# An LRU scan gated by a GEGLU network on one core: the engine orders are planned anew, with a charge between dependent neighbours on one engine

## The chip, the cores and the metric

The kernel runs on one core of a Trainium2 chip. The core's engines work side by side, each through its own queue, in order: TensorE (PE in the profile; its weight loads are PEld), VectorE (DVE), ScalarE (ACT) and GpSimd (POOL); SyncE (SP) issues most of the DMAs, ScalarE and GpSimd issue a few. Engines wait for one another on semaphores. The metric is the device time of one execution in microseconds, lower is better; of several runs the median is taken.

## The reference

`x` is 2048 tokens of 512 numbers in bfloat16. The reference normalizes it, sends it through a complex diagonal recurrence (512 states, one step per token) and through a GEGLU network of width 1376, and joins the two with `x`:

```python
def _A_ref(x, Lambda_re, Lambda_im, B_re, B_im, C_re, C_im, log_dt, Dskip):
    Lam = Lambda_re + 1j * Lambda_im
    Bmat, Cmat = B_re + 1j * B_im, C_re + 1j * C_im
    dt = jnp.exp(log_dt)
    Lam_bar = jnp.exp(dt * Lam)
    B_bar = ((Lam_bar - 1.0) / Lam)[:, None] * Bmat
    Bu = jnp.einsum("bld,pd->blp", x + 0j, B_bar)
    h = jnp.zeros_like(Bu[:, 0, :])
    hs = []
    for t in range(L):
        h = Lam_bar[None, :] * h + Bu[:, t, :]
        hs.append(h)
    hseq = jnp.stack(hs, 1)
    return 2.0 * jnp.einsum("blp,dp->bld", hseq, Cmat).real + x * Dskip[None, None, :]

def _B_ref(x, w_gate, w_up, w_down):
    return (_gelu(x @ w_gate) * (x @ w_up)) @ w_down

xn = _layernorm(x, axis=-1)
s = _A_ref(xn, ...)
g = _silu(_B_ref(xn, ...))
return x + s * g
```

## The kernel before, in words

**Tiles and stages.** The 2048 tokens are cut into four stretches (s = 0 to 3) of 512, each of four tiles (m) of 128 tokens. For each stretch the kernel makes:

- the normalized tile xn and its transpose xnT. For s = 0 and 1 VectorE takes statistics (`stats`, L375 and L377; `rstd`, L383; GpSimd's power, L380; `norm_dve`, L417); for s = 2 and 3 ScalarE sums x and its square (L764, into junk), VectorE works out four small operations (L769 to L772) and nb (L775), and ScalarE writes xn (L746). The transposes of s = 0 go through TensorE (L398, evicted by ScalarE, L401), those of the other stretches through SP's DMA queue (L423);
- the gate and up products (TensorE, L450 for s = 0, L471 after), evicted by ScalarE as gelu (gt) and copy (ub), multiplied by VectorE into at (L457; L489 and L491), transposed by DMA into atT (L497);
- the state input (L573), in two halves of the states, evicted by ScalarE into U (L576); then on VectorE, for each half: Q = U times a table of cosines and sines (L587), W = sum of two parts of Q (L599; L595 for s = 0), four real scans Fs (L606), the carry ini (L616 to L619), Q = Fs times the table (L587) and hst (L599). This turns the complex recurrence into real scans in a rotating frame;
- the down product from atT and wd (L514), evicted by ScalarE through silu into g (L518);
- the y product from hst and C (`y_tile`, L533). It is accumulated in one of two PSUM banks (ybank). Before it ScalarE writes the skip term sk (made by VectorE, L427) into the bank as the start value (L529, the seed); the first two y tiles have no seed and add sk on VectorE (L543, tF). VectorE multiplies the bank by g (L539 yg; L545 for the first two), adds x (L547 ot), and SP sends ot out (L550). A bank may be seeded for its next tile once yg (or tF) has read it.

TensorE has three more double banks in PSUM (slot), taken in turn by gate and up, state and down products. It may write a bank again when ScalarE has evicted it.

**The order.** The kernel is written as a list of steps, each with an engine, a cost, what it reads and writes. `Plan` orders them: some passes of list scheduling, then 3000 trials with random changes of the starts (seeded, so the same list always gives the same order), each judged by a model: every engine takes one step after the other, a step begins when what it needs is ready, and the best order by `goal` is what the program then issues. TensorE's steps are chained to one another and keep the order in which they are written. The cost of a VectorE step is `base + n / 960 / rate`, with 0.072 for `base` where nothing is given. A step that depends on another engine's step begins that step's lag later (0.13 for VectorE, 0.15 for ScalarE, 0.22 for TensorE); one that depends on its own engine's step begins when that ends:

```python
def _same(self, i, u):
    a, b = min(i, u), max(i, u)
    return a in self.steps[b][8] or (self.steps[a][0] == self.steps[b][0] and self.steps[a][0] in (PE, DVE, ACT, POOL))
...
    e = t + cost + (0.0 if same else lag if forward else self.steps[u][4])
```

No step of the plan is timed at run time: the plan's costs decide the order alone.

Of the kernel before, what the change touches and what calls it, by code (L numbers as in the profile page):

```python
# [13 lines left out]
ALU = mybir.AluOpType  # L14
# [6 lines left out]
PE, ACT, DVE, POOL, SP, ACTQ = "PE", "ACT", "DVE", "POOL", "SP", "ACTQ"  # L21


class Plan:
# [9 lines left out]
    def add(self, eng, cost, emit, reads=(), writes=(), lag=0.05, table=None, not_before=0.0, rank=0.0, after=()):  # L34
        n = len(self.steps)
        deps = set()
        for k in reads:
            if k in self.wrote:
                deps.add(self.wrote[k])
        for k in writes:  # L40
            if k in self.wrote:
                deps.add(self.wrote[k])
            deps.update(self.read.get(k, ()))
        deps.update(after)
        if eng == PE:
            if self.last_pe is not None:
                deps.add(self.last_pe)
            self.last_pe = n
        for k in reads:
            self.read.setdefault(k, []).append(n)  # L50
        for k in writes:
            self.wrote[k] = n
            self.read[k] = []
        deps.discard(n)
        self.steps.append((eng, cost, emit, sorted(deps), lag, table, not_before, rank, frozenset(after)))
        return n

    def _same(self, i, u):

        a, b = min(i, u), max(i, u)  # L60
        return a in self.steps[b][8] or (self.steps[a][0] == self.steps[b][0] and self.steps[a][0] in (PE, DVE, ACT, POOL))

    def _pass(self, into, prio, forward):


        n = len(self.steps)
        out = [[] for _ in range(n)]
        for i in range(n):
            for d in into[i]:
                out[d].append(i)  # L70
        left = [len(into[i]) for i in range(n)]
        ready_at = [self.steps[i][6] if forward else 0.0 for i in range(n)]
        waiting = {}
        free = {}
        loaded = None
        start = [None] * n
        for i in range(n):
            if left[i] == 0:
                waiting.setdefault(self.steps[i][0], []).append(i)
        done = 0  # L80
        length = 0.0
        while done < n:
            t, eng = min((max(free.get(e, 0.0), min(ready_at[i] for i in w)), e) for e, w in waiting.items() if w)
            w = waiting[eng]
            ahead = LOOK if eng in (DVE, ACT, POOL) else 1e-9

            def value(i):
                v = prio[i] - HOLD * max(0.0, ready_at[i] - t)
                table = self.steps[i][5]
                if table is not None and table != loaded:  # L90
                    v -= TABLE
                return (v, -i)

            i = max((j for j in w if ready_at[j] <= t + ahead), key=value)
            w.remove(i)
            t = max(t, ready_at[i])
            cost, lag, table = self.steps[i][1], self.steps[i][4], self.steps[i][5]
            if table is not None and table != loaded:
                loaded = table
                cost = cost + 1.3  # L100
            start[i] = t
            free[eng] = t + cost
            length = max(length, t + cost + (lag if forward else 0.0))
            done += 1
            for u in out[i]:
                same = self._same(i, u)
                e = t + cost + (0.0 if same else lag if forward else self.steps[u][4])
                ready_at[u] = max(ready_at[u], e)
                left[u] -= 1
                if left[u] == 0:  # L110
                    waiting.setdefault(self.steps[u][0], []).append(u)
        return start, length

    def _decode(self, users, key):

        n = len(self.steps)
        left = [len(s[3]) for s in self.steps]
        ready_at = [s[6] for s in self.steps]
        heap = [(key[i], i) for i in range(n) if left[i] == 0]
        heapq.heapify(heap)  # L120
        free = {}
        loaded = None
        start = [0.0] * n
        length = 0.0
        while heap:
            i = heapq.heappop(heap)[1]
            eng, cost, _, _, lag, table = self.steps[i][:6]
            t = max(free.get(eng, 0.0), ready_at[i])
            if table is not None and table != loaded:
                loaded = table  # L130
                t = max(t, free.get(eng, 0.0) + 1.3)
            start[i] = t
            free[eng] = end = t + cost
            length = max(length, end + lag)
            for u, same in users[i]:
                e = end if same else end + lag
                if e > ready_at[u]:
                    ready_at[u] = e
                left[u] -= 1
                if left[u] == 0:  # L140
                    heapq.heappush(heap, (max(key[u], key[i]), u))
        return start, length

    def run(self):
        n = len(self.steps)
        deps = [s[3] for s in self.steps]
        users = [[] for _ in range(n)]
# [2 lines left out]
                users[d].append(i)  # L150
        tail = [0.0] * n
        for i in range(n - 1, -1, -1):
            eng, cost, lag = self.steps[i][0], self.steps[i][1], self.steps[i][4]
            tail[i] = cost + max((tail[u] + (0.0 if self._same(i, u) else lag) for u in users[i]), default=0.0)
        rank = [s[7] for s in self.steps]
        best = None
        prio = tail
# [12 lines left out]
            back, _ = self._pass(users, [start[i] + self.steps[i][1] for i in range(n)], False)  # L170
            prio = [back[i] + self.steps[i][1] for i in range(n)]
        rng = random.Random(1)
        pairs = [[(u, self._same(i, u)) for u in users[i]] for i in range(n)]
        for r in range(TRIALS):
            key = list(best[1])
            if r:
# [16 lines left out]
def kernel(  # L193
# [34 lines left out]
    MAGIC = 12582912.0  # L228
# [3 lines left out]
    V, A, G, T = nc.vector, nc.scalar, nc.gpsimd, nc.tensor  # L232
# [33 lines left out]
    sk = [sb(f"sk{i}", [P, M, D]) for i in range(2)]  # L266
    NG2 = 3
    g2 = [sb(f"g2_{i}", [P, 2, D], FP32) for i in range(NG2)]
    yg = [sb(f"yg{i}", [P, D]) for i in range(2)]
# [12 lines left out]
    def dve(n, emit, reads=(), writes=(), rate=1.0, base=DV, **kw):  # L282
        return pl.add(DVE, base + n / 960.0 / rate, emit, reads, writes, lag=0.13, **kw)
# [89 lines left out]
    def stats(s, m):  # L373
        def f():
            V.bn_stats(out=st[:, s, m, :], in_=x_tok[:, s * M + m, :])  # L375
        dve(512, f, [("x", s, m)], [("st", s, m)], base=0.1)
        dve(6, lambda: V.bn_aggr(out=mv[:, s, m, :], in_=st[:, s, m, :]), [("st", s, m)], [("mv", s, m)], base=0.17)  # L377

    def power(out, base, exponent, n, reads, writes):
        pool(0.45 + 0.2 * n, lambda: G.tensor_tensor(out=out, in0=base, in1=exponent, op=ALU.pow), reads, writes)  # L380

    def rstd(s, a, b):
        dve(b - a, lambda: V.tensor_scalar(out=ve[:, s, a:b], in0=mv[:, s, a:b, 1], scalar1=EPS, scalar2=None, op0=ALU.add),  # L383
            [("mv", s, m) for m in range(a, b)], [("ve", s, m) for m in range(a, b)], base=0.14)
        power(rs[:, s, a:b], ve[:, s, a:b], mhalf[:, a:b], b - a, [("ve", s, m) for m in range(a, b)] + ["mhalf"], [("rs", s, m) for m in range(a, b)])

    def dummies(k, i):
# [135 lines left out]
    def y_tile(s, m):  # L523
# [13 lines left out]
        gi, b = g2s[s, m]  # L537
        if seed:
            dve(512, lambda: V.tensor_tensor(out=yg[e][:], in0=bank[:], in1=g2[gi][:, b, :], op=ALU.mult),  # L539
                [("y", i), ("g2", gi)], [("yg", e)])  # L540
        else:
            ys = tF[:, i, :]
            dve(512, lambda: V.tensor_tensor(out=ys, in0=bank[:], in1=sk[s % 2][:, m, :], op=ALU.add),  # L543
                [("y", i), ("sk", s % 2, m)], [("tF",)])
            dve(512, lambda: V.tensor_tensor(out=yg[e][:], in0=ys, in1=g2[gi][:, b, :], op=ALU.mult),  # L545
                [("tF",), ("g2", gi)], [("yg", e)])
        dve(512, lambda: V.tensor_tensor(out=ot[e][:], in0=yg[e][:], in1=x_tok[:, s * M + m, :], op=ALU.add),  # L547
            [("yg", e), ("x", s, m)], [("ot", e)], rate=2.0)
        mg = s * TS + m * P
# [73 lines left out]
    def tables():  # L623
# [1 line left out]
        sh, ch = sb("sh", [P, NPT, NB]), sb("ch", [P, NPT, NB])  # L625
        sp, cp = sb("sp", [P, NPT, NA, 2]), sb("cp", [P, NPT, NA, 2])
        dve(196, lambda: V.tensor_tensor(out=ang[:], in0=iota_f[:].unsqueeze(1).to_broadcast(W3), in1=thn.unsqueeze(2).to_broadcast(W3), op=ALU.mult),
            ["iota", "thn"], ["ang"], base=0.13)
        dve(196, lambda: V.tensor_scalar(out=kr[:], in0=ang[:], scalar1=MAGIC, scalar2=MAGIC, op0=ALU.add, op1=ALU.subtract), ["ang"], ["kr"], rate=2.0, base=0.13)
        dve(196, lambda: V.tensor_tensor(out=ang[:], in0=ang[:], in1=kr[:], op=ALU.subtract), ["kr"], ["ang", "kr"], base=0.13)  # L630
        dve(196, lambda: V.scalar_tensor_tensor(out=kr[:], in0=ang[:], scalar=-1.0, in1=ang[:], op0=ALU.mult, op1=ALU.max), ["ang"], ["kr"], base=0.13)
        early.append(acts(196, lambda: act(out=sbt[:], in_=ang[:], func=AF.Sin, scale=TWO_PI), ["ang"], ["sbt"], table="silu", rank=20.0))
        early.append(acts(196, lambda: act(out=cbt[:], in_=kr[:], func=AF.Sin, scale=-TWO_PI, bias=halfpi[:]), ["kr", "halfpi"], ["cbt", "trig"], table="silu", rank=20.0))
# [218 lines left out]
```

## Time and profile before

| what | value |
|---|---|
| median of 8 runs | 184.9 us |
| fastest and slowest run | 183.1 and 185.41 us |
| the profiled execution, its own time | 183.19 us |
| its span, first to last instruction | 181.4 us |
| TensorE busy in the span | 174.3 us (96%) |
| VectorE busy | 159.2 us (88%) |
| ScalarE busy | 117.8 us (65%) |
| GpSimd busy | 11.9 us (7%) |
| mean granted TensorE clock | 0.996 |

The eight runs in order: 184.93, 183.1, 183.23, 185.41, 185.36, 184.87, 185.3, 183.26.

How to read the profile: a row of the timeline gives the start and the duration in us, the engine, the line of the kernel, the operation, out<-in by the kernel's names (buffer numbers left out), shapes, and how many instructions were merged. In brackets stands idle time of the engine ahead of the row and what ended it. The end of a matmul is modelled and overlaps the next one's start, so starts are what to go by. The two durations of VectorE's neighbours may overlap a little: the next one starts while the one ahead is finishing.

### The profile page before, as it was taken

Reading aid. Unit: us, or ns where it says so; the run is one execution under the profiler, and the core shown is the slowest. Engines: PE = TensorE matmul, PEld = TensorE weight load, DVE = VectorE, ACT = ScalarE, POOL = GpSimd, SP = SyncE. Lnnn points to the kernel's source line nnn. Section 1 sums busy time; section 2 is a strip of 40 time slices with the busy share of each in tenths; the row PEclk is TensorE's granted clock in tenths of the full one; section 3 lists DMA queues with packets and bytes.
Section 4 is the critical chain, followed back from the end, with each engine's and each line's share of the span. In section 5 each row is a group of like instructions: output and inputs, shape, how many; then the busy total and the mean of one; then the engine's idle time right before and its main releaser. Section 6 shows DMA issues by size and latency. Waiting matters only on the chain.

```text
span 181.4 us, 2388 instructions
## 1 busy us (share of the span) xinstructions
PE 174.3 (96%) x848; PEld 82.5 (45%) x848; DVE 159.2 (88%) x265; ACT 117.8 (65%) x178; POOL 11.9 (7%) x21
## 2 busy tenths in 40 slices
PE   6999999999999999999999999999999999799990
PEld 2454445544444545444444544444444545344440
DVE  5899899999999999999999999999999999840072
ACT  4599699698999998565289774347428666242220
POOL 5430331000000200000020000000000000000000
PEclk9999999999999999999999999999999999999998
DMA  4999999991000577400020673041000241830011
GB/s 123 376 305 227 361 146 242 267 230 25 0 0 0 98 146 102 91 0 0 9 79 33 124 148 68 14 83 60 29 29 0 57 88 32 155 102 5 0 58 58
DMA packets 46995, 18.01 MB, mean 99 GB/s; under 512 B 38440, under 2 KB 46984, under 8 KB 46984
## 3 DMA queue, kind: packets, MB, share of 16 engines
q1 hardware_dynamic: 46400, 17.34, 42.4%
q10 hardware_dynamic: 552, 0.53, 1.1%
q8 instruction: 6, 0.10, 0.2%
q14 instruction: 5, 0.04, 0.1%
q0 software_dynamic: 32, 0.00, 0.0%
HBM read 6.33 MB, written 2.10 MB: 46 GB/s over the span
## 4 chain that ended last, share of the span: by engine, by line
DVE 73%; PE 12%; issue 6%; DMA 3%; POOL 2%; ACT 1%; SPq 1%; DVEq 0%
DVE Fs L606 20%; DVE Q L587 18%; PE ybank L533 6%; PE slot L514 5%; DVE W L599 4%; DVE at L489 4%; DMA wu<-in_B_w_up_dram 3%; DVE hst L599 3%; DVE yg L539 3%; DVE sk L427 2%; DVE Q L647 2%; DVE at L457 2%; DVE ot L547 2%; DVE at L491 2%; DVE C L790 2%
## 5 line engine op out<-in xcount | busy, mean ns | idle before, releaser
L471 PEld LDWEIGHTS <-xnT 128*128 128x128 bf16 x288 | 28.2, 98 | 28.4
L514 PE MATMUL slot<-wd,atT 128*128 128x512 bf16 (+1 forms) x176 | 38.7, 379 | 0.0
L471 PE MATMUL slot<-wg,xnT 128*128 128x512 bf16 (+1 forms) x144 | 31.8, 357 | 0.0
L471 PE MATMUL slot<-wu,xnT 128*128 128x512 bf16 (+1 forms) x144 | 31.8, 357 | 0.0
L533 PE MATMUL ybank<-C,hst 128*128 128x512 bf16 x128 | 28.9, 379 | 1.3 <-ACT ybank L529 1.3
L606 DVE TENSOR_TENSOR_SCAN Fs<-rho,ini,W 128x512 bf16<-128x512 f32 x24 | 29.3, 1268 | 0.1
L573 PE MATMUL slot<-xnT,BT 128*128 128x512 bf16 x128 | 28.3, 379 | 0.0
L514 PEld LDWEIGHTS <-atT 128*128 128x128 bf16 (+1 forms) x176 | 17.2, 98 | 20.9
L576 ACT ACTIVATE U<-slot 128x1024 bf16<-128x1024 f32 x16 | 16.1, 1020 | 11.1 <-PE slot L573 11.1
L539 DVE TENSOR_TENSOR yg<-ybank,g 128x512 bf16<-128x512 f32 x14 | 9.7, 690 | 13.9 <-PE ybank L533 13.5
L529 ACT ACTIVATE ybank<-sk 128x512 f32<-128x512 bf16 x14 | 8.4, 601 | 18.2 <-DVE yg L539 17.1
L533 PEld LDWEIGHTS <-hst 128*128 128x128 bf16 x128 | 12.5, 98 | 15.8 <-issue 1.6
L573 PEld LDWEIGHTS <-BT 128*128 128x128 bf16 x128 | 12.5, 98 | 15.0
L587 DVE TENSOR_TENSOR Q<-U,tab 128x4096 bf16<-128x4096 bf16 x8 | 18.3, 2289 | 0.4
L587 DVE TENSOR_TENSOR Q<-Fs,tab 128x4096 bf16<-128x4096 bf16 x8 | 18.3, 2291 | 0.2
L518 ACT ACTIVATE g<-slot 128x1024 f32<-128x1024 f32 x8 | 8.1, 1018 | 13.1 <-PE slot L514 13.1
L479 ACT ACTIVATE gt<-slot 128x1024 bf16<-128x1024 f32 x12 | 12.2, 1018 | 2.9 <-PE slot L471 2.9
L479 ACT ACTIVATE ub<-slot 128x1024 bf16<-128x1024 f32 x12 | 12.3, 1022 | 2.4 <-PE slot L471 2.2
L450 PEld LDWEIGHTS <-xnT 128*128 128x128 bf16 x96 | 9.2, 97 | 8.7 <-issue 0.2
L450 PE MATMUL slot<-wu,xnT 128*128 128x512 bf16 (+1 forms) x44 | 10.2, 355 | 0.1
L450 PE MATMUL slot<-wg,xnT 128*128 128x512 bf16 (+1 forms) x44 | 10.2, 355 | 0.0
L764 ACT ACTIVATE junk<-x_tok 128x512 bf16<-128x512 bf16 x16 | 10.0, 626 | 0.2
(117 smaller groups left out, 180.6 us busy)
## 6 DMA issues: line engine op xcount, KB each, us to landing
out_dram<-ot SPq DMA_DIRECT2D x16, 128.0 KB, 1.7
x_tok<-in_A_x_dram SPq DMA_DIRECT2D x3, 512.0 KB, 7.0
wd<-in_B_w_down_dram SPq DMA_DIRECT2D x1, 1280.0 KB
wu<-in_B_w_up_dram SPq DMA_DIRECT2D x2, 512.0 KB, 5.6
x_tok<-in_A_x_dram SPq DMA_DIRECT2D x4, 128.0 KB, 3.3
wg<-in_B_w_gate_dram ACTq DMA_DIRECT2D x1, 512.0 KB, 4.8
wg<-in_B_w_gate_dram SPq DMA_DIRECT2D x1, 512.0 KB, 6.5
wg<-in_B_w_gate_dram SPq DMA_DIRECT2D x1, 352.0 KB, 4.1
```

The lines of the kernel that those rows point to most:

```text
L450: T.matmul(pss[bank][:, 0:w], lhsT=xnT[:, k, t0 : t0 + P], rhs=wt[:, k, a:b], start=(k == 0), stop=(k == KT - 1))
L471: T.matmul(ps[:, bank, 0 : b - a], lhsT=xnT[:, k, t0 : t0 + P], rhs=wt[:, k, a:b], start=(k == 0), stop=(k == KT - 1))
L479: acts(1024, lambda ps=ps, dst=dst, fn=fn: act(out=dst[:, 0:1024].rearrange("p (c w) -> p c w", c=2), in_=ps[:, :, :], func=fn), [("slot", ...
L514: T.matmul(ps[:, b, :], lhsT=atT[:fs, k, m * P : (m + 1) * P], rhs=wd[:fs, k, :], start=(k == 0), stop=(k == NFT - 1))
L533: T.matmul(bank[:, :], lhsT=hst[s % 2][:, j // NPT, j % NPT, m * P : (m + 1) * P], rhs=C2[:, j // NPT, j % NPT, :], start=(j == 0 and not ...
L539: dve(512, lambda: V.tensor_tensor(out=yg[e][:], in0=bank[:], in1=g2[gi][:, b, :], op=ALU.mult), [("y", i), ("g2", gi)], [("yg", e)])
L573: T.matmul(ps[:, ri, :], lhsT=BT[:, ri, k, pt * P : (pt + 1) * P], rhs=xnT[:, k, (s % 2) * TS : (s % 2 + 1) * TS], start=(k == 0), stop=(k ...
L576: acts(1024, lambda q=q, ps=ps: act(out=U[ui][:, :, q, :], in_=ps[:, :, :], func=AF.Copy), [("slot", i, 0), ("slot", i, 1)], [("U", ui, q)])
L587: dve(4096, lambda: V.tensor_tensor(out=Qf, in0=src.unsqueeze(1).to_broadcast(WQ), in1=table, op=ALU.mult), reads, ["Q"], rate=2.0)
L599: dve(2048, lambda: V.tensor_tensor(out=dst, in0=Qf[:, 0, :, :], in1=Qf[:, 1, ::-1, :], op=ALU.add), ["Q"], writes, rate=2.0)
L606: pl.add(DVE, 1.116 if s == 0 else 1.19, lambda ri=ri, q=q, pt=pt, first=first: V.tensor_tensor_scan(out=Fs[:, ri, q, :], data0=rho[:, pt ...
L764: acts(512, lambda i=i, fn=fn, m=m: act(out=junk[:], in_=x_tok[:, s * M + m, :], func=fn, accum_out=sx[:, s, i, m : m + 1]), [("x", s, m)] ...
```

## The change

The diff touches the planner and the costs that it is given, and no instruction:

- Two dependent steps on one engine: a VectorE, ScalarE or GpSimd step that reads what a step of its own engine wrote now begins 0.11 us after that step's end in the model. TensorE's steps, and steps that only overwrite what their engine's step read or wrote, begin at once, as before. The set of steps whose results are read is kept apart for this (`raw`). In the backward pass the lag now taken is that of the earlier step.
- Costs: the steps of the y tile (L539, L543, L545) have 0.13 for `base` where they had 0.072; `bn_stats` 0.12 for 0.1; `bn_aggr` 0.08 for 0.17; L383 0.072 for 0.14; three of the four operations on the table's angles (L627, L629, L630) 0.072 for 0.13.

```diff
@@ Plan.add
+        raw = frozenset(deps)
         for k in writes:
             if k in self.wrote:
                 deps.add(self.wrote[k])
...
-        self.steps.append((eng, cost, emit, sorted(deps), lag, table, not_before, rank, frozenset(after)))
+        self.steps.append((eng, cost, emit, sorted(deps), lag, table, not_before, rank, frozenset(after), raw))

-    def _same(self, i, u):
-
-        a, b = min(i, u), max(i, u)
-        return a in self.steps[b][8] or (self.steps[a][0] == self.steps[b][0] and self.steps[a][0] in (PE, DVE, ACT, POOL))
+    def _lag(self, a, b):
+
+        if a in self.steps[b][8]:
+            return 0.0
+        if self.steps[a][0] == self.steps[b][0] and self.steps[a][0] in (PE, DVE, ACT, POOL):
+            return 0.11 if self.steps[a][0] != PE and a in self.steps[b][9] else 0.0
+        return self.steps[a][4]

@@ Plan._pass
-                same = self._same(i, u)
-                e = t + cost + (0.0 if same else lag if forward else self.steps[u][4])
+                e = t + cost + self._lag(min(i, u), max(i, u))

@@ Plan._decode
-            for u, same in users[i]:
-                e = end if same else end + lag
+            for u, wait in users[i]:
+                e = end + wait

@@ Plan.run
-            tail[i] = cost + max((tail[u] + (0.0 if self._same(i, u) else lag) for u in users[i]), default=0.0)
+            tail[i] = cost + max((tail[u] + self._lag(i, u) for u in users[i]), default=0.0)
...
-        pairs = [[(u, self._same(i, u)) for u in users[i]] for i in range(n)]
+        pairs = [[(u, self._lag(i, u)) for u in users[i]] for i in range(n)]

@@ stats, rstd
-        dve(512, f, [("x", s, m)], [("st", s, m)], base=0.1)
-        dve(6, lambda: V.bn_aggr(...), [("st", s, m)], [("mv", s, m)], base=0.17)
+        dve(512, f, [("x", s, m)], [("st", s, m)], base=0.12)
+        dve(6, lambda: V.bn_aggr(...), [("st", s, m)], [("mv", s, m)], base=0.08)
...
-            [("mv", s, m) for m in range(a, b)], [("ve", s, m) for m in range(a, b)], base=0.14)
+            [("mv", s, m) for m in range(a, b)], [("ve", s, m) for m in range(a, b)])

@@ y_tile (three steps alike)
-                [("y", i), ("g2", gi)], [("yg", e)])
+                [("y", i), ("g2", gi)], [("yg", e)], base=0.13)

@@ tables (three steps alike)
-            ["iota", "thn"], ["ang"], base=0.13)
+            ["iota", "thn"], ["ang"])
```

The built program has the same instructions. TensorE's order is the same throughout. On the other engines the orders differ in many places; line numbers here and in the prediction are those of the kernel before (the changed kernel's are three higher from `_pass` on). Those that the text below speaks of:

- VectorE, start: L383 of tile 1 stands behind the statistics of tile 2; the fourth statistics stand ahead of xn of tile 1.
- VectorE, 12 to 27 us: two at products stand behind the input of the four-wide power (L383) and behind the xn that wait for the power; two sk products (L427) of s = 1 stand among the table's steps, which stood after 59 us.
- VectorE, from the first scans on: other work stands between many pairs of neighbours of which the second reads the first (Q, W, scans, hst), for example an at product or an ot.
- VectorE, around the second tF (L543, 72 us): one scan that stood behind it stands ahead, and at of one tile (L489, L491) behind it.
- ScalarE: the second copy of tab (L655) stands ahead of the third eviction of U (L576), and three junk passes ahead of the fifth; a tF of the C stage (L785) stands between the second g of s = 0 (L518) and the gelu table's load (L479); at 83 us the silu table's load stands behind two seeds (L529) instead of ahead of them.
- SP: the last 96 rows of wd (L696) are loaded behind the four xnT transposes of s = 1 instead of ahead of them; some transposes of at and xn have changed places.
- GpSimd: sh is cast ahead of ch (L635).

More of the change, by code (lines that the diff above doesn't have):

```diff
@@ L152, in run @@
         for i in range(n - 1, -1, -1):
-            eng, cost, lag = self.steps[i][0], self.steps[i][1], self.steps[i][4]
-            tail[i] = cost + max((tail[u] + (0.0 if self._same(i, u) else lag) for u in users[i]), default=0.0)
+            cost = self.steps[i][1]
+            tail[i] = cost + max((tail[u] + self._lag(i, u) for u in users[i]), default=0.0)
         rank = [s[7] for s in self.steps]
@@ L375, in f @@
             V.bn_stats(out=st[:, s, m, :], in_=x_tok[:, s * M + m, :])
-        dve(512, f, [("x", s, m)], [("st", s, m)], base=0.1)
-        dve(6, lambda: V.bn_aggr(out=mv[:, s, m, :], in_=st[:, s, m, :]), [("st", s, m)], [("mv", s, m)], base=0.17)
+        dve(512, f, [("x", s, m)], [("st", s, m)], base=0.12)
+        dve(6, lambda: V.bn_aggr(out=mv[:, s, m, :], in_=st[:, s, m, :]), [("st", s, m)], [("mv", s, m)], base=0.08)
     def power(out, base, exponent, n, reads, writes):
@@ L543, in y_tile @@
             dve(512, lambda: V.tensor_tensor(out=ys, in0=bank[:], in1=sk[s % 2][:, m, :], op=ALU.add),
-                [("y", i), ("sk", s % 2, m)], [("tF",)])
+                [("y", i), ("sk", s % 2, m)], [("tF",)], base=0.13)
             dve(512, lambda: V.tensor_tensor(out=yg[e][:], in0=ys, in1=g2[gi][:, b, :], op=ALU.mult),
-                [("tF",), ("g2", gi)], [("yg", e)])
+                [("tF",), ("g2", gi)], [("yg", e)], base=0.13)
         dve(512, lambda: V.tensor_tensor(out=ot[e][:], in0=yg[e][:], in1=x_tok[:, s * M + m, :], op=ALU.add),
@@ L627, in tables @@
         dve(196, lambda: V.tensor_tensor(out=ang[:], in0=iota_f[:].unsqueeze(1).to_broadcast(W3), in1=thn.unsqueeze(2).to_broadcast(W3), op=ALU.mult),
-            ["iota", "thn"], ["ang"], base=0.13)
-        dve(196, lambda: V.tensor_scalar(out=kr[:], in0=ang[:], scalar1=MAGIC, scalar2=MAGIC, op0=ALU.add, op1=ALU.subtract), ["ang"], ["kr"], rate=2.0, base=0.13)
-        dve(196, lambda: V.tensor_tensor(out=ang[:], in0=ang[:], in1=kr[:], op=ALU.subtract), ["kr"], ["ang", "kr"], base=0.13)
+            ["iota", "thn"], ["ang"])
+        dve(196, lambda: V.tensor_scalar(out=kr[:], in0=ang[:], scalar1=MAGIC, scalar2=MAGIC, op0=ALU.add, op1=ALU.subtract), ["ang"], ["kr"], rate=2.0)
+        dve(196, lambda: V.tensor_tensor(out=ang[:], in0=ang[:], in1=kr[:], op=ALU.subtract), ["kr"], ["ang", "kr"])
         dve(196, lambda: V.scalar_tensor_tensor(out=kr[:], in0=ang[:], scalar=-1.0, in1=ang[:], op0=ALU.mult, op1=ALU.max), ["ang"], ["kr"], base=0.13)
```

## Prediction

> **What bounds the kernel now.** I read the engine shares first, then TensorE's timeline from end to end, then the list of waits, and then VectorE and ScalarE around the one hole that this left. The shares:
>
> ```profile
> PE 174.3 (96%) x848; PEld 82.5 (45%) x848; DVE 159.2 (88%) x265; ACT 117.8 (65%) x178; POOL 11.9 (7%) x21
> ```
>
> TensorE's timeline shows group behind group from 8.26 us on: each starts where the one before has issued its columns (four 512-column matmuls every 0.86 us, so 0.216 each). There is one hole:
>
> ```profile
> 152.39 3.62 PE L533 MATMUL ybank<-C,hst 128*128 128x512 bf16 x16
> 157.27 3.61 PE L533 MATMUL ybank<-C,hst 128*128 128x512 bf16 x16 [1.27 <-ACT ybank L529]
> ```
>
> The first 16 are issued by 152.39 + 16 x 0.216 = 155.84; the next start at 157.27. The hole is 1.43 us (1.27 of it after the last result has left the array). Nothing follows that could win it back: 44 down products, 32 y products, the last output. A microsecond of hole is a microsecond of the end. The hole is VectorE's doing:
>
> ```profile
> 154.72 0.68 DVE L489 TENSOR_TENSOR at<-gt,ub 128x1024 bf16<-128x1024 bf16 x1
> 155.32 0.33 DVE L491 TENSOR_TENSOR at<-gt,ub 128x352 bf16<-128x352 bf16 x1
> 155.57 0.42 DVE L427 TENSOR_TENSOR sk<-xn,Drow 128x512 bf16<-128x512 bf16 x1
> 155.90 0.69 DVE L539 TENSOR_TENSOR yg<-ybank,g 128x512 bf16<-128x512 f32 x1
> 156.62 0.60 ACT L529 ACTIVATE ybank<-sk 128x512 f32<-128x512 bf16 x1 [3.22 <-DVE yg L539]
> ```
>
> yg must empty the bank, ScalarE seeds it, then TensorE may write: 157.27 is yg's start plus 1.37. To close the hole yg must start by 155.84 - 1.37 = **154.47**. VectorE's row has no idle stretch marked between 20 and 158 us; it is late because it is full. So TensorE bounds the kernel, and VectorE's queue makes the one hole in it.
>
> **What two neighbours on VectorE cost.** The same timeline:
>
> ```profile
> 146.19 0.67 DVE L489 TENSOR_TENSOR at<-gt,ub 128x1024 bf16<-128x1024 bf16 x1
> 146.77 0.34 DVE L491 TENSOR_TENSOR at<-gt,ub 128x352 bf16<-128x352 bf16 x1
> 147.02 2.46 DVE L606 TENSOR_TENSOR_SCAN Fs<-rho,ini,W 128x512 bf16<-128x512 f32 x2
> 149.51 2.29 DVE L587 TENSOR_TENSOR Q<-Fs,tab 128x4096 bf16<-128x4096 bf16 x1
> ```
>
> An independent neighbour starts 0.084 before the one ahead ends (146.86, next at 146.77); one that reads what its neighbour wrote starts 0.034 after (149.48, then 149.51). A dependent pair costs **0.118** more. Where the second also waits for another engine and overwrites what its neighbour read, the gap is 0.104 (ot ends 89.66, yg at 89.76), 0.188 more.
>
> [...]
>
> **The change, part by part.** It runs the same instructions. TensorE's order is the same to the last matmul; only VectorE, ScalarE, SP and GpSimd are ordered anew.
>
> *VectorE from the second tF (L543) to the late yg.* Before: 72.21 to 155.90, 83.69 us. In the new order, counted in that stretch: neighbours that read their neighbour's result fall from 19 to 9 (10 x 0.118 = 1.18); gaps of 0.104 from 6 to 4 (2 x 0.188 = 0.38); one more overwrites what its neighbour read (+0.12); one scan (issue 1.18) now stands ahead of tF and one tile's two at products (0.60 + 0.25) behind it (-0.33). Sum -1.77.
>
> The start of the stretch can't move: tF needs the y product of 70.28, and a y product is readable 1.93 after its start (157.27, then yg at 159.20): 72.21. By the same counting (two sk products moved ahead, two dependent pairs and one overwrite fewer, the scan put before) VectorE reaches tF at about 71.6 and waits 0.6: **what the change wins before 72 us is given back there**. So yg comes at 72.21 + 83.69 - 1.77 = 154.13, before 154.47. By then the bank must be full: 152.39 + 1.93 = 154.32, which is the later. The next y products can start at 154.32 + 1.37 = 155.69, before 155.84. **The hole closes: -1.43**, with 0.34 us to spare on VectorE and 0.15 on the bank.
>
> *Start.* Tile 1's L383 moves behind tile 2's statistics, which wait for x until 6.00. So xn of tile 1 starts about 7.62 instead of 7.01 (behind the fourth statistics), and its transposes 8.08 instead of 7.76. Behind them in TensorE's queue stand the wu matmuls, held until 8.26 by the load of wu; four transposes take 0.23, so they start 8.31. Cost **+0.05**; without wu's load as cover +0.3.
>
> *GpSimd.* sh is cast ahead of ch, and their reader waits for both: 11.95 as before. The four-wide power of L380 starts some 0.7 earlier, because two at products no longer stand ahead of its input; it ends about 19.0, not 19.64, and xn's wait shrinks from 0.58 to 0.3. Into the room come two sk products (0.67), so the first Q from U starts about 0.1 later than 26.96.
>
> *ScalarE, first half.* The copy of tab goes ahead of an eviction:
>
> ```profile
> 27.25 1.02 ACT L576 ACTIVATE U<-slot 128x1024 bf16<-128x1024 f32 x1 [0.47 <-PE slot L573]
> 28.17 1.90 ACT L655 ACTIVATE tab<-tab 128x2048 bf16<-128x2048 bf16 x1
> 29.97 0.76 PE L450 MATMUL slot<-wg,xnT 128*128 128x352 bf16 x4
> ```
>
> The copy waits for VectorE's tab (26.86 + 0.1), starts 27.0; the eviction starts 1.80 later and ends 29.82; TensorE wants that bank at 29.97. Cost 0, with 0.1 to spare (before: 1.7). The three junk passes moved ahead of another eviction need x, landed 34.46: 34.55 + 3 x 0.75, then 1.02, ends 37.8; the bank is wanted 38.73. Cost 0.
>
> *ScalarE, 50 to 55.* The table load of L479 now follows a tF (1.05), while the g ahead of it starts 50.2, not 51.05, two junk passes having gone before. Its end: 51.2 + 1.05 + 1.28 + 1.02 = 54.6; TensorE wants the bank at 54.62 and starts about 0.05 after a release. Cost 0 to 0.2, taken **+0.05** (the nearest row: seed's end 157.22, matmul 157.27).
>
> *ScalarE, 83 to 97.* The silu table load goes behind two seeds; VectorE's second yg there comes 88.8 instead of 90.89. Seed 89.5, table, two g, gelu table, gt: done 95.6; bank wanted 96.53. Cost 0.
>
> *SP.* The last 96 rows of wd (issued 16.42, landed 24.56) go behind the four xnT transposes of 1.2 to 1.3 each. Those start at xn's end, 19.4; wd follows near 25, and the C transposes keep their 25.3. Even at its old 8.1 us wd lands at 33; the first down product to read it issues ten matmuls after 40.46. Later swaps of xnT and atT leave 5 us or more to their readers. Cost 0.
>
> **Sum.** -1.43 + 0.05 + 0.05 = **-1.33**: span 181.41 to 180.1, this execution 183.19 to 181.9. The profiled execution is near the fastest of the runs; the median is 184.9. The hole closes in both, so 184.9 - 1.3 = **183.6 us**, 0.7% less. One per cent (1.85 us) is about what a measurement of this kernel tells from no change.
>
> **Rivals.**
>
> *The hole closes in part* (0.2). [...]
>
> *More than the hole* (0.2). The runs reach from 183.1 to 185.41 and the profile tells of a short one. If the others are longer because VectorE stands later at this yg, the hole is larger there and the full 1.77 or more counts: 183.0 or below. Against: the one trace can't show it.
>
> *Slower* (0.1): the silu table load behind the seeds. Before it was hidden at 83.61, behind no seed. Now yg, seed, table 1.28, g, g, table, gt are one chain to the bank at 96.53, with 0.9 to spare. Each microsecond by which that yg comes later than 89.7 stops TensorE for one; it costs more than the gain when yg passes 91.0, 2.2 us later than I have it. Then some 186.9 if it is 4.2 late. Against: yg's operands (a product of 75 us, g) are long there; only VectorE's own queue could be that late.
>
> **How the numbers follow.** The main case has 0.5, its own range 183.3 to 184.0. The range to 2 in 10 left out takes in the partial case and most of the larger gain: 182.0 to 185.2. Faster by over 1% (below 183.05): the larger gain and a tenth of the main case, 0.26. Slower by over 1%: the table chain and a little for a second hole unseen, 0.12. The rest, 0.62, is within 1%.
>
> **What would show it.** Right: no hole over 0.2 at the y products near 155 us; the late yg at about 154.4; VectorE waiting some 0.6 at the second tF near 72; wu's first group at 8.3; every later group in TensorE's row earlier only from 155.8 on. Wrong: a wait of TensorE at 29.97, 54.6 or 96.5 for ScalarE; a VectorE wait after 72; dependent and independent neighbours with one gap.

## The result, and the profile after

The changed kernel's median is 181.8 us (21 runs, 181.49 to 183.92), that of the kernel before, run beside it, 184.92 (56 runs). The median is below the predicted 183.6 and just below the range, which began at 182.0. The ratio of the two kernels is given as 0.9888 (95% interval 0.986 to 0.9917). It is not that of the two medians, 0.983: it weighs both of the levels described next and comes out as that of the runs' means. By it the change is 1.1%, where 0.7% was forecast, and 184.9 would become 182.8.

The 3.1 us between the medians are not what the change is worth. Runs of both kernels fall on two levels some 1.9 us apart. Over all sets of runs in this study the kernel before has 150 near 183.17 and 83 near 185.09, the changed kernel 33 near 181.78 and 10 near 183.52. Slow runs, over 1.5% above the fastest of their kernel, are left out of such counts throughout (eleven of the kernel before, at 186.47 to 187.23). Level against level the change is worth **1.4 and 1.6 us**, 0.8%. The rest is how many runs of each set fell on which level: the eight runs shown before had five on the upper one, the changed kernel's 21 also had five. What makes the levels is shown below.

The profiled execution took 181.67 us (183.19 before), its span 179.9 (181.4). Both are on the lower level. From the page of the changed kernel, the shares of the engines and the chain that ended last:

```profile
PE 173.7 (97%) x848; PEld 82.5 (46%) x848; DVE 157.2 (87%) x265; ACT 117.6 (65%) x178; POOL 12.0 (7%) x21
...
PE 93%; DMA 2%; DVE 2%; SPq 0%; issue 0%
```

VectorE has the same 265 instructions and is busy 2 us less. Their durations sum to 175.0 us in both traces; more of them now start while the one ahead is still finishing. The chain is TensorE's almost alone. Before, it ran 73% over VectorE, from the hole at 155 us back. TensorE's timeline of the changed kernel:

```profile
152.27 7.07 PE L536 MATMUL ybank<-C,hst 128*128 128x512 bf16 x32
159.18 9.68 PE L517 MATMUL slot<-wd,atT 128*128 128x512 bf16 x44
```

The two groups of 16 y products are one of 32, and 152.27 + 32 x 0.216 = 159.18: the hole of 1.43 is gone to the last hundredth. Nothing else moved on TensorE: matmul by matmul (848, in the same order) the starts are 0.11 earlier from wu's first group on (8.15 for 8.26) and 1.55 earlier from the second 16 of these y products on (152.27 + 16 x 0.216 = 155.73 for 157.27). VectorE's timeline shows how:

```profile
72.10 0.69 DVE L546 TENSOR_TENSOR tF<-ybank,sk 128x512 f32<-128x512 f32 x1 [0.68 <-PE ybank L536]
...
73.31 2.29 DVE L590 TENSOR_TENSOR Q<-Fs,tab 128x4096 bf16<-128x4096 bf16 x1
75.51 0.33 DVE L494 TENSOR_TENSOR at<-gt,ub 128x352 bf16<-128x352 bf16 x1
75.76 1.22 DVE L602 TENSOR_TENSOR hst<-Q 128x2048 bf16<-128x2048 bf16 x1
...
153.64 0.34 DVE L494 TENSOR_TENSOR at<-gt,ub 128x352 bf16<-128x352 bf16 x1
154.20 0.69 DVE L542 TENSOR_TENSOR yg<-ybank,g 128x512 bf16<-128x512 f32 x1 [0.22 <-PE ybank L536]
```

Q ends at 75.60 and at starts at 75.51, before that end; at ends at 75.84 and hst starts at 75.76. With at between them, the pair Q, hst costs no gap. VectorE waits 0.68 us for the second tF, so the winnings ahead of it are given back there; and it is ready for the late yg 0.22 before the bank is, at 153.98.

### The profile page after: what moved, and what is told of

It is laid out like the page before. It is cut to its first block, busy times and chain, and to the rows that moved or that the text cites. A ratio compares the mean times of both kernels' runs of the same rounds, so it can differ in the third digit from the quotient of the medians.

```text
span 179.9 us, 2398 instructions
## 1 busy us (share of the span) xinstructions
PE 173.7 (97%) x848; PEld 82.5 (46%) x848; DVE 157.2 (87%) x265; ACT 117.6 (65%) x178; POOL 12.0 (7%) x21
## 4 chain that ended last, share of the span: by engine, by line
PE 93%; DMA 2%; DVE 2%; SPq 0%; issue 0%
PE slot L474 31%; PE slot L517 21%; PE ybank L536 15%; PE slot L576 15%; PE slot L453 9%; DMA x_tok<-in_A_x_dram 2%; PE ybank L453 1%; DVE st L378 1%; PE ybank L401 0%; SPq L320 0%; DVE yg L542 0%; DVE ot L550 0%; DVE xn L420 0%; DVE ve L386 0%; DVE mv L380 0%
## 5 line engine op out<-in xcount | busy, mean ns | idle before, releaser
L576 PE MATMUL slot<-xnT,BT 128*128 128x512 bf16 x128 | 28.3, 379 | 0.0
L576 PEld LDWEIGHTS <-BT 128*128 128x128 bf16 x128 | 12.5, 98 | 15.0
L453 PE MATMUL slot<-wg,xnT 128*128 128x512 bf16 (+1 forms) x44 | 10.2, 355 | 0.0
L453 PE MATMUL slot<-wu,xnT 128*128 128x512 bf16 (+1 forms) x44 | 10.2, 355 | 0.0
```

What stands on the lines that cost most here:

```text
L453: T.matmul(pss[bank][:, 0:w], lhsT=xnT[:, k, t0 : t0 + P], rhs=wt[:, k, a:b], start=(k == 0), stop=(k == KT - 1))
L576: T.matmul(ps[:, ri, :], lhsT=BT[:, ri, k, pt * P : (pt + 1) * P], rhs=xnT[:, k, (s % 2) * TS : (s % 2 + 1) * TS], start=(k == 0), stop=(k ...
```

## The experiments

All times are read level against level where medians mix. The lower level is 183.17 for the kernel before and 181.78 for the changed kernel. The first four kernels vary the planner, the next three move steps by hand in a finished order, the last five look into TensorE's first microseconds (one of them is the changed kernel once more).

**The charge alone, and the costs alone.**

```diff
# e_charge: the changed kernel with the costs of before, for instance
-                [("y", i), ("g2", gi)], [("yg", e)], base=0.13)
+                [("y", i), ("g2", gi)], [("yg", e)])
# e_costs: the kernel before with the new costs, without _lag and raw
```

> The charge of 0.11 alone, with the costs of before. Theory (parted neighbours close the hole): counted with the gaps of the trace of before, VectorE comes to the late yg at 154.3, TensorE's hole at the y products near 156 is 0 to 0.1, and the span is within 0.2 us of the changed kernel's 179.9. Rival (the costs made the new order, the charge does nothing by itself): hole about 1.4, span about 181.4.

Measured: span 179.9, ratio 0.9918 (0.9884 to 0.9952), lower level 181.81. The rows of VectorE, then TensorE:

```profile
154.27 0.69 DVE L542 TENSOR_TENSOR yg<-ybank,g 128x512 bf16<-128x512 f32 x1
154.88 1.22 DVE L602 TENSOR_TENSOR hst<-Q 128x2048 bf16<-128x2048 bf16 x1
```

```profile
152.34 7.07 PE L536 MATMUL ybank<-C,hst 128*128 128x512 bf16 x32
```

No hole. yg comes at 154.27, which is when the bank becomes readable (152.34 + 1.93 = 154.27); VectorE's work ahead of it ends at 154.23, so VectorE was there in time, as counted (154.3). This plan takes a way of its own: 17 of the 19 dependent pairs are left, and the last hst stands behind the yg. Two pairs fewer are worth 0.24 us, the hst put off 1.1. The charge alone makes the whole gain, but here more by the order than by parted pairs.

> The new costs alone, no charge. Theory: the same counting gives 15 dependent neighbours left of 19 between the second tF and the late yg, but the second tF 0.7 us late (72.9); the late yg at 155.0, a hole of about 0.6, span about 180.5. Rival (the costs made the new order): no hole, span 179.9.

Measured: ratio 0.999 (0.995 to 1.003), span 181.8. Both theories missed. The hole at the y products is gone, but TensorE has three others, and together they cost what was won: the time is that of before. Two of them are marked, and ScalarE's rows show the second:

```profile
12.38 1.02 PE L450 MATMUL slot<-wg,xnT 128*128 128x512 bf16 x4 [0.88 <-ACT Drow L679]
98.37 1.89 PE L471 MATMUL slot<-wg,xnT 128*128 128x512 bf16 x8 [0.51 <-ACT gt L479]
```

```profile
95.17 0.81 ACT L746 ACTIVATE xn<-x_tok,nb,rs 128x512 bf16<-128x512 bf16 x1 [0.76 <-DVE nb L775]
96.00 1.28 ACT L479 ACT_TABLE_LOAD   x1
97.30 1.02 ACT L479 ACTIVATE gt<-slot 128x1024 bf16<-128x1024 f32 x1
```

Against the kernel before, TensorE's starts fall back 0.95 at 11.50 (an eviction of ScalarE), 0.28 at the y products of 73.74 (VectorE comes to the second tF at 73.53) and 0.67 at 96.53. There ScalarE waits for nb, then writes xn, and only then loads the gelu table for the gt that must empty the bank. The last y products then come at 157.68, where 157.27 + 0.95 + 0.28 + 0.67, less 0.06 for an earlier start, is 159.11: 1.43 less, the hole. VectorE was ready for the late yg at 155.80 and waited for the bank:

```profile
156.15 0.69 DVE L539 TENSOR_TENSOR yg<-ybank,g 128x512 bf16<-128x512 f32 x1 [0.35 <-PE ybank L533]
```

155.80 is after the deadline of before, 154.47, but TensorE's own delays had moved the deadline to 156.31. So it was TensorE's lateness that closed this hole.

**Other seeds of the plan's random trials.**

```diff
-        rng = random.Random(1)
+        rng = random.Random(3)
```

> The kernel before with another seed of the plan's random trials (3 for 1). Theory: without the charge the plan has no reason to part dependent neighbours: 19 of them stay, the late yg at 155.8, hole about 1.3, span about 181.2. Rival (the gain was a lucky draw of the search): the hole changes with the seed and could be gone here, span anywhere from 179.9 up.

Measured: ratio 1.0005 (0.997 to 1.004), lower level 182.95. The profile, one of the upper level, has the hole:

```profile
154.20 3.62 PE L533 MATMUL ybank<-C,hst 128*128 128x512 bf16 x16
158.80 1.45 PE L533 MATMUL ybank<-C,hst 128*128 128x512 bf16 x6 [0.98 <-ACT ybank L529]
```

The 16 y products from 154.20 are issued by 157.66, the next start at 158.80: 1.14 us. Nearly the loss of before, from another draw.

> The changed kernel with another seed (3 for 1). Theory: 11 dependent neighbours, VectorE ready for the late yg at 153.7, so that yg waits for the bank; no hole, span within 0.2 us of 179.9. Rival (a lucky draw): a hole comes back, here or at another bank, span 180.5 or more.

Measured: span 180.0, no hole, lower level 181.85, ratio 0.9938 (0.9905 to 0.9972). The late yg waits 0.20 for its bank, where it waited 0.22 with seed 1. The hole is there in both draws without the charge and in neither with it. That speaks against luck of the search; two draws on each side can't rule it out.

**The gain by another road: four sk products out of the way.** In the planned order of VectorE, step x goes behind step y (counted from 0), and the other engines keep theirs; lines are 26 higher than in the kernel before.

```diff
+MOVES = [(203, 217), (204, 203), (205, 204), (209, 205)]
...
+        for x, y in [(vec[x], vec[y]) for x, y in MOVES]:
+            vec.remove(x)
+            vec.insert(vec.index(y) + 1, x)
```

> The kernel before, with one edit of VectorE's order alone: the four sk products of the last stretch, which stood ahead of the late yg and whose results are wanted only after 160 us, go behind the last ot of the third stretch. No dependent pair is parted. If the hole is all that the gain is made of, whatever brings yg earlier gives it: yg at 155.90 - 4 x 0.336 = 154.56, TensorE on at 155.93, a hole of 0.1, span about 180.1. If the gain has another source too (fewer dependent neighbours elsewhere), the span stays above 180.5 though the hole is gone.

Measured: span 180.1, six runs of 181.49 to 181.92, ratio 0.9887 (0.9832 to 0.9943). VectorE, then TensorE:

```profile
154.62 0.68 DVE L568 TENSOR_TENSOR yg<-ybank,g 128x512 bf16<-128x512 f32 x1
```

```profile
152.46 7.14 PE L562 MATMUL ybank<-C,hst 128*128 128x512 bf16 x32
```

yg at 154.62 where 154.56 was counted, and the y products run through but for 0.07 (7.14 for 7.07). With all 19 dependent pairs left as they were, one edit in VectorE's order wins what the change wins. So the gain is the hole and nothing else, and dependent pairs matter only as one way to bring this yg forward.

**The changed kernel with its pairs put back.** The same edit on the changed kernel (lines 29 higher), thirteen moves that set nine pairs side by side:

```diff
+MOVES = [(126, 127), (141, 142), (159, 161), (172, 173), (176, 177), (151, 152), (191, 194), (193, 191), (201, 206), (202, 201), (203, 202), (204, 203), (205, 204)]
```

> The changed kernel, with nine pairs of dependent VectorE neighbours between 79 and 152 us put side by side again (what stood between them goes behind the second), nothing else moved. Theory: 8 x 0.118 + 0.188 = 1.13 us later at the late yg, 153.98 + 1.13 = 155.1; a hole of 0.65, span about 180.5. Rival (a dependent neighbour costs nothing; other moves of the order made the gain): yg still at 154.2, no hole, span 179.9.

Measured: ratio 0.9959 (0.9927 to 0.9992), lower level 182.56, 0.8 above the changed kernel. Its profile is one of the upper level, with everything on TensorE 1.94 later from the start on. VectorE, then TensorE:

```profile
150.50 2.29 DVE L619 TENSOR_TENSOR Q<-Fs,tab 128x4096 bf16<-128x4096 bf16 x1
152.83 1.23 DVE L631 TENSOR_TENSOR hst<-Q 128x2048 bf16<-128x2048 bf16 x1
...
157.02 0.68 DVE L571 TENSOR_TENSOR yg<-ybank,g 128x512 bf16<-128x512 f32 x1
```

```profile
154.21 3.62 PE L565 MATMUL ybank<-C,hst 128*128 128x512 bf16 x16
158.38 3.61 PE L565 MATMUL ybank<-C,hst 128*128 128x512 bf16 x16 [0.55 <-ACT ybank L561]
```

hst again starts 0.04 after Q's end (152.79). From the second tF (74.04) to the late yg it is 82.98 us; the changed kernel needed 81.88 (72.10 to 153.98). The difference is **1.10**, counted 1.13 (eight pairs at 0.118 and one, hst and the Q that overwrites what it read and waits for U, at 0.188). The hole is back with 158.38 - (154.21 + 16 x 0.216) = 0.71, expected 0.65. Dependent neighbours do cost what the rows of before say.

**The start's order.**

```diff
+MOVES = [(16, 17), (21, 22)]
```

> The changed kernel, with the start's VectorE order of before: L386 of tile 1 ahead of the statistics of tile 2, xn of tile 1 ahead of the fourth statistics. xn of tile 1 about 7.0 instead of 7.36, its transposes 7.6 instead of 7.81. If the load of wu sets TensorE's start (the 0.11 that the changed kernel won there was the load's landing, not the order), the first wu group stays 0.04 behind that landing, near 8.1 to 8.3, and the time is that of the changed kernel within 0.1. If the transposes set it, the group starts 0.2 earlier.

Measured: lower level 181.73, within 0.1 of the changed kernel's 181.78; ratio 0.9935 (0.9904 to 0.9966). Its profile fell on the upper level, so the row of wu can't be read off there. But in four other profiles of the lower level wu's first group stands 0.04 us behind wu's landing (8.11 and 8.15 in the changed kernel; 8.22 and 8.26 before; 8.18 and 8.22; 8.30 and 8.34). There the load sets the start. It does not always: in the changed kernel with seed 3, which has the same order there, x landed at 5.97 (5.72 with seed 1), and TensorE waited for the transposes, with wu there since 8.15:

```profile
8.06 0.40 PE L401 MATMUL ybank<-ident,xn 128*128 128x128 bf16 x4 [0.20 <-DVE xn L420]
8.30 1.03 PE L453 MATMUL slot<-wu,xnT 128*128 128x512 bf16 x4
```

So the new order can cost 0.1 there when x comes late. On the medians of the lower level it costs no more than 0.05.

**What the two levels are.** The changed kernel, profiled once more, fell on the upper one.

> The changed kernel once more, beside the three below. Its runs fall on two levels, near 181.75 and 183.6; three profiles of other kernels that fell on the upper level show every TensorE start from the first wu group on 1.8 to 2.0 us later, and matmuls of 512 columns at 0.427 instead of 0.216 us apart until 10.3 to 10.5, where profiles of the lower level change at 4.4 to 5.7. Expected: about two thirds of the runs at 181.75, most of the rest at 183.6.

Measured: ratio 0.993 (0.9903 to 0.9957); 17 of 22 runs on the lower level. TensorE's start in the changed kernel's first profile:

```profile
2.90 1.98 PE L393 MATMUL slot<-junk 128*128 128x512 bf16 x5
5.16 0.40 PE L401 MATMUL ybank<-ident,xn 128*128 128x128 bf16 x4 [0.28 <-DVE xn L420]
...
6.35 1.02 PE L453 MATMUL slot<-wg,xnT 128*128 128x512 bf16 x4
...
8.15 1.02 PE L453 MATMUL slot<-wu,xnT 128*128 128x512 bf16 x4
```

and in the second, the same program:

```profile
2.90 2.34 PE L393 MATMUL slot<-junk 128*128 128x512 bf16 x5
5.20 0.61 PE L401 MATMUL ybank<-ident,xn 128*128 128x128 bf16 x4
...
7.10 1.91 PE L453 MATMUL slot<-wg,xnT 128*128 128x512 bf16 x4
...
9.88 1.16 PE L453 MATMUL slot<-wu,xnT 128*128 128x512 bf16 x4
```

Four wg products take 1.02 in the one, 1.91 in the other: 512 columns are 0.216 apart there, 0.427 here, half the rate. The first profile goes to the full rate between 4.2 and 4.5 us, the second between 9.9 and 10.2. From then on every start is 1.87 later, to the y products (154.14 for 152.27). The two changes of rate are 5.7 us apart in two runs of one program, and no view shows what sets the moment. Behind the first junk matmuls TensorE has a thin stretch: transposes, 4x4 products and one junk matmul, from 5.20 to 7.10 in the second profile. Four kernels ask whether the junk matmuls bear on the moment: one has fewer, three have more.

```diff
# e_warm_half: half of the first eight junk matmuls
-            for _ in range(k):
+            for _ in range(k // 2 if k == 8 else k):
```

> The changed kernel with 4 instead of 8 of the junk matmuls that TensorE runs before its first work. [...] Rival (the levels come from the loads or from elsewhere): shares as in the changed kernel.

Measured: all 22 runs at 183.43 to 184.94, median 184.13, ratio 1.002 (0.9995 to 1.0044). None is on the lower level, where 17 of 22 of the changed kernel were. The profile shows the half rate until past 12:

```profile
10.07 1.91 PE L453 MATMUL slot<-wu,xnT 128*128 128x512 bf16 x4
...
12.21 1.32 PE L453 MATMUL slot<-wg,xnT 128*128 128x512 bf16 x4
13.36 1.03 PE L453 MATMUL slot<-wu,xnT 128*128 128x512 bf16 x4
```

```diff
# e_warm_early: VectorE's memset of junk first; nine junk matmuls for eight
+MOVES = [(0, 7), (1, 0), (2, 1), (3, 2), (4, 3), (5, 4), (6, 5)]
...
-            for _ in range(k):
+            for _ in range(k + (k == 8)):
# e_warm_dense: also two more junk matmuls behind the first transposes
+                for _ in range(2):
+                    T.matmul(slots[0][:, 0, :], lhsT=warm[:, 0:P], rhs=warm[:], start=True, stop=True)
# e_before_warm: the edits of e_warm_early in the kernel before
```

> The changed kernel with VectorE's memset of junk ahead of its seven other memsets (the junk matmuls can start 0.3 us earlier) and nine junk matmuls for eight. [...]

> As the run with nine junk matmuls, and two more behind the first transposes, where TensorE has only small products and waits until 6.3 us. [...] Median 181.8 to 182.0, no runs at 183.6. Rival: two levels as before.

> The kernel before, with the same two edits of the start (VectorE's memset of junk ahead of its other memsets, nine junk matmuls for eight). Theory: the two losses are independent. The hole of 1.43 stays, so the lower level stays at 183.1 to 183.2; fewer runs than the third of the kernel before lie at 185. Rival (the early memset of the changed kernel only drew lucky runs): the share at 185 is as in the kernel before.

Measured: with the early memset six runs, all at 181.46 to 181.97, ratio 0.9886 (0.9836 to 0.9935). Six of six may be chance where two thirds fall there anyway, and in the kernel before the same edits give no sign of a better share: 15 runs near 183.2 and 6 near 185.1, beside 18 and 9 of the kernel before in the same set, ratio 0.9995 (0.9961 to 1.003). The early memset is not shown to help; the first junk matmul came only 0.2 earlier (1.44 for 1.64).

With the two more in the thin stretch no run is on the upper level: all 14 lie at 181.68 to 182.7, none at 183.6; the ratio is 0.9914 (0.9884 to 0.9944). They have the early memset and the ninth junk matmul too, but these alone gave no better share in the kernel before. The profile:

```profile
5.68 1.06 PE L433 MATMUL slot<-junk 128*128 128x512 bf16 x2
...
7.46 1.03 PE L485 MATMUL slot<-wg,xnT 128*128 128x512 bf16 x4
...
8.97 1.03 PE L485 MATMUL slot<-wu,xnT 128*128 128x512 bf16 x4
```

The junk pair is slow (1.06), wg at 7.46 is fast. But wu stands at 8.97, 0.8 behind 8.15, about what two products take at the half rate (2 x 0.427 = 0.85): TensorE has no wait marked from the first transposes on, and the pair itself holds it from 5.68 to 6.67. The median of 182.22 is no better than the 181.88 that the changed kernel had beside it. The spread is smaller, the time isn't. No version tried is shown to beat the changed kernel.

## Why the prediction was right, and where it was wrong

- **The bound and the hole: right.** The hole closed by 1.43, as said. From the second tF to VectorE's readiness for yg it was 81.88, predicted 83.69 - 1.77 = 81.92. The wait at the second tF is 0.68, predicted 0.6; the bank was readable at 154.20, predicted 154.32, on a TensorE 0.11 earlier.
- **0.118 for a dependent neighbour: right.** Nine pairs put back cost 1.10 of 1.13 counted.
- **The rival of a hole that closes in part did not come.** No run shows a reason for it: the hole closed by 1.43 of 1.43, VectorE had no wait at the late yg but the 0.22 for its bank, and dependent pairs cost what was counted.
- **The start: mis-sized.** Predicted +0.05 because tile 1's transposes would come at 8.08; measured -0.11. The statistics of tile 2 began at 5.74, not 6.00, as x landed earlier in this run; xn of tile 1 came at 7.36, its transposes at 7.81. wu landed at 8.11 for 8.22, and at 8.4 in the changed kernel's second profile: that 0.11 is the run's, not the change's. The mechanism was right: with seed 3, where x landed at 5.97, the transposes came at 8.06 and wu's first group at 8.30, predicted 8.08 and 8.31.
- **ScalarE at 50 to 55: mis-sized.** Predicted +0.05, measured 0: gt ended at 53.43 + 1.02 = 54.45 and TensorE took the bank at 54.50, in step with its own earlier start.
- **GpSimd and the first Q: mis-sized, at no cost.** The four-wide power ended at 18.40, not 19.0, and the first Q from U came at 26.70, not 27.06. TensorE's row shows neither.
- **The sum.** -1.33 was predicted for the span, -1.55 measured: -1.43 and the 0.11 of the start. For the profiled execution 181.9 was predicted; it took 181.67.
- **The median: wrong.** The step that failed is "the hole closes in both, so 184.9 - 1.3 = 183.6". The hole does close in both (the kernel before with seed 3, profiled on the upper level, has it with 1.14). But a median over two levels jumps with their shares. From 183.1, the lower level in the eight runs shown, the same sum gives 181.8.
- **The rival of more than the hole: wrong in its mechanism.** Its number, 183.0 or below, is what the median did, and that is luck. It had longer runs with VectorE later at this yg. They are longer in the first 10 us, on TensorE, and no run here shows that the change touches that.
- **The slow rival did not come.** ScalarE's gt for the bank at 96.53 ended at 95.52, predicted 95.6. The place was well chosen all the same: the plan with new costs alone lost 0.67 there, to the gelu table's load behind an xn that waited for nb.
- **Not foreseen:** that the charge without the costs would do, and that the costs without the charge open as much as they close.

## What to carry to other kernels

Find the one hole of the bounding engine and the one instruction that it waits for, and work out by when that must start; any move that brings it there wins the hole and no more, be it ten parted pairs or four products put off. Dependent neighbours on VectorE (here 0.118 us a pair) are worth parting only ahead of such an instruction. Before a median is predicted, look whether the runs fall on levels, and predict the level: here two levels made 3.1 us of a change worth 1.5.

## What the runs showed of the hardware

- The granted clock of the profile does not show the slow start. Its mean is 0.996 in the changed kernel's first profile and 0.997 in the second, which ran at half rate for 5.7 us longer. The spacing of equal matmuls shows it: 0.427 or 0.216 us for 512 columns.
- With eight junk matmuls from 1.6 us the full rate came between 4.2 and 5.7 us in the profiles of the lower level and between 9.9 and 10.6 in those of the upper; with four it came near 12.8 in the one profile, and no run of 22 was on the lower level; with eleven, two of them behind the transposes, by 6.7. What sets the moment is not shown, nor why the shares were 77% to 23% in the changed kernel's sets and 64% to 36% in those of the kernel before. Over the changed kernel and four that differ from it little at the start (the charge alone, seed 3, pairs back, the start's order) 42 of 125 runs are on the upper level, 34%. The kernel before had 29 of 53 there in its first set and 54 of 180 in the four later ones, so the share moves with the set, and a difference by the change is not shown.
- In the trace of before an independent neighbour on VectorE starts 0.084 us before the one ahead ends, a dependent one 0.034 after it. In that of the changed kernel one operation between two dependent ones hid the gap whole: the 352-column at (0.33 us) between Q and hst.
